# Gated linear attention, top-1 experts and a gated MLP: steps around the last head pair in another order, and widths by count for the first expert

## The chip, the cores and the metric

The kernel runs on one NeuronCore of a Trainium2 chip. The metric is the device time of one execution in microseconds (us), a median of three runs. The core has TensorE (PE, with its weight loads shown apart as PEld), VectorE (DVE), ScalarE (ACT), GpSimd (POOL) and the sync engine (SP), which only issues DMAs.

## The reference

```python
# 4 batches x 8 heads, 768 steps, head dim 48
for t in range(S):
    state = alpha[:, :, t, :, None] * state + np.einsum('bhd,bhe->bhde', k[:, :, t], v[:, :, t])
    y[:, :, t] = np.einsum('bhd,bhde->bhe', q[:, :, t], state)
x = y as (3072 tokens, 384)
# 8 experts, each token to one of them
logits = x @ w_gate
expert_idx = np.argmax(logits, axis=1); gate_w = softmax(logits)[expert_idx]
h = np.maximum(xe @ w1[e], 0.0); out[mask] = gate_w[mask, None] * (h @ w2[e])   # D=384, F=1024
# a second MLP over all tokens
h = x @ w_in; g = h * (1.0 / (1.0 + np.exp(-h))); result = g @ w_out            # 384 -> 2048 -> 384
```

All inputs and outputs are float32. With the reference's inputs, experts 0 to 7 get 420, 387, 356, 354, 404, 409, 352 and 390 tokens.

## The kernel before, in words

The program order on each engine is written out by hand; nothing is rescheduled. Eight PSUM banks (0 to 7) are given out by number.

**Attention.** The 32 heads are 16 pairs `p` (four to a batch), and the 768 steps are six chunks of 128. The loop over `p` runs to 16; each pass begins pair `p` and ends pair `p - 1`. For a pair, `scores` (tile `Ap`) and a mask give the part within a chunk; `ks_transpose` and `updates` give each chunk's update of the state; `states(p)` scans these on VectorE (tile `So`) and ScalarE copies the result to `Sb`; `from_states` and `within` add both parts up in PSUM (tile `Yp`, two halves of three chunks), and `y_copy(p, 0)` and `y_copy(p, 1)`, the "sums", copy the halves to `xb`. Named places in the pass (`"F1"`, `"F2"`, `"F3"`, `"U"`, `"C1"`, `"C2"`) take further steps from a table, through `aside(p, place)`. After the last pair of a batch, `logits(b)` multiplies the batch's `xb` with the gate's weights (tile `Lp`): eight fp32 matmuls, recorded as 16 passes, in four groups of 32 columns of the array. The sixth and the eighth of the matmuls read the last pair's halves. `route(b)` then finds each token's expert.

**Experts.** Tokens of an expert are gathered from DRAM (`xg`), transposed (`x_tile`, `x_rows`) and split into a high part `xh` (ScalarE) and a low part `xl` (VectorE). Weights come as tiles of 128x768, t = 0 to 7 for expert 0, and so on; `w_split(t)` casts one on ScalarE to `wh` and subtracts on VectorE or GpSimd to `wl`. A slice's first product `F1` is nine matmuls (hi·hi, lo·hi, hi·lo for three parts of the rows) into a bank `hp`; ScalarE makes `hh`, VectorE `hl` from it, and nine matmuls of `S1` add to three banks `yb` (two of them are also called `both`). Expert 0 goes in two passes: slices 0 to 5 on its first 192 columns, whose tokens come from the first three batches, while the last batch is being routed; then

```python
seq = [(t, CA, CAPS[0]) for t in range(part)] + [(t, 0, CAPS[t // NF]) for t in range(part, E * NF)]
```

that is, columns 192 to 448 of slices 0 to 5, slices 6 and 7 on all 448, and then the other experts, larger ones first. Slices of `seq` go in pairs; the first products run one slice ahead.

For experts 1 to 7, `sized(e, body)` loads the expert's count into a register of TensorE and chooses by comparisons, one after the other, among four widths (`ARMS[e]`); each width has its own copy of the matmuls. Expert 0 has no such choice: it runs at 448. Columns of `hp` that a narrower arm doesn't write have to be zero, so `hold()` takes three banks for good and clears them, after the sixth slice of `seq`:

```python
HB[0] = -1
for i in HBS:
    t = bank(i, [128, CAP], "hp")
    nc.vector.memset(t, 0.0)
    held.append(t)
```

At the end of the attention loop (`p` = 16), the steps stand in this order: `x_rows` of the first two gathered tiles, `within`, `y_copy(15, 0)` on ScalarE, `y_copy(15, 1)` on VectorE, `w_split(2)`, `w_split(3)`, `logits(3)`.

Of the kernel before, what the change touches and what calls it, by code (L numbers as in the profile page):

```python
# [9 lines left out]
F32 = mybir.dt.float32  # L10
# [12 lines left out]
NP = B * H // 2  # L23
# [15 lines left out]
ARMS = [  # L39
    [448],  # L40
    [420, 432, 444, 464],
# [198 lines left out]
def gla_moe_kernel(  # L240
# [87 lines left out]
    def w_load(t):  # L328
# [9 lines left out]
        nc.sync.dma_start(raw[t], wt[ds(wbase[r] + f, 1)].rearrange("o p f -> (o p) f"))  # L338

    def w_split(t, eng=nc.vector):  # L340
        hi, lo = wslot[slot1(t)]
        nc.scalar.copy(hi, raw[t])  # L342
        eng.tensor_tensor(lo, raw.pop(t), hi.bitcast(F32), op=ALU.subtract)  # L343

# [40 lines left out]
    turn = const.tile([128, E, E], F32, name="turn")  # L385
    regs = const.tile([128, 24], I32, name="regs")

# [11 lines left out]
    with actx:  # L399
# [252 lines left out]
        def states(p):  # L652
# [9 lines left out]
            if 0 < p < NP - 1:  # L662
                y_copy(p - 1, 0)
            for h in range(2):
                r = slice(64 * h, 64 * h + D)
                dst = Sb[p % 2][r, 1:NC, 64 * h : 64 * h + D]
                src = so[r].rearrange("p e c -> p c e")[:, 1:NC, :]
                if p == NP - 1 and h:
                    nc.vector.tensor_copy(dst, src)
                else:  # L670
                    nc.scalar.copy(dst, src)
# [33 lines left out]
        def y_copy(p, g):  # L705
            b, i = p // 4, p % 4
            if g == 0 and i == 0:
                xb[b] = xp.tile([PA, 4, S], F32, tag="xb", name="xb")
            c0 = 3 * g * CH
            dst, src = xb[b][:, i, c0 : c0 + 3 * CH], st[p]["y", g].rearrange("p c t -> p (c t)")  # L710
            if p == NP - 1 and g:
                nc.vector.tensor_copy(dst, src)
            else:
                nc.scalar.copy(dst, src)

# [250 lines left out]
        def beside_pairs(b):  # L966
# [23 lines left out]
            else:  # L990
# [7 lines left out]
                    (p + 2, "F2"): [invert, add, gather_a],  # L998
                    (p + 2, "C2"): [lambda: w_split(0, nc.gpsimd), lambda: w_split(1), lambda: w_load(4)],
                }  # L1000
# [28 lines left out]
        for p in range(NP + 1):  # L1029
# [49 lines left out]
            if not on:  # L1079
                x_rows(XG[0], XS[0], 0, 0, 128, bank(2, [128, KD, 128], "xt"))  # L1080
                x_rows(XG[1], XS[0], 1, 0, CA - 128, bank(0, [128, KD, 128], "xt"))
            if oy:
                within(p - 1, 0)
                within(p - 1, 1)
            if p < NP - 1:
                states(p)
            if p >= NP - 1:
                y_copy(p - 1, 0)
            if oy:
                y_copy(p - 1, 1)  # L1090
# [9 lines left out]
            if not on:  # L1100
                w_split(2)
                w_split(3)
                logits(B - 1)
# [20 lines left out]
    with mctx:  # L1124
# [126 lines left out]
        def hold():  # L1251

            HB[0] = -1
            for i in HBS:
                t = bank(i, [128, CAP], "hp")
                nc.vector.memset(t, 0.0)  # L1256
                held.append(t)

# [7 lines left out]
        def F1_inner(t, c0, c1):  # L1266
# [7 lines left out]
            )  # L1274
            hq[t, c0] = (hh, hl)

        yb = {}
# [51 lines left out]
        for t in range(part):  # L1329
            if t == 2:  # L1330
                add()
                w_split(4)
                gather(0, (1, 2, 3))
                for t_ in yb.values():
                    nc.vector.memset(t_[:, CAPS[0] :], 0.0)  # L1335
            if t == 3:
# [10 lines left out]
            if t == 0:  # L1347
                row[5]()
                for step in placed:
                    step()  # L1350
        x_tile(0, 3, bk=3)
        for t in range(4, 6):
            next_load()
        soon = [6, 7]
        HB[0], HBS[:] = -1, [5, 6, 3]
        F1(*seq[0])
        lctx.close()
# [9 lines left out]
        def offsets():  # L1367
# [7 lines left out]
            nc.vector.tensor_copy(regs[:, 9:16], cnt[:, 1:E])  # L1375

        count = {}

        def sized(e, body):

            if e not in count:
                c = 8 + e if e else 8
                count[e] = nc.values_load(regs[0:1, c : c + 1], engines=(ET.PE,), min_val=0, max_val=NT)

            def arm(i):
                if i == len(ARMS[e]) - 1:
                    body(ARMS[e][i])
                    return
                with tc.If(count[e] <= ARMS[e][i]) as cmp:
                    body(ARMS[e][i])  # L1390
                with cmp.Else():
                    arm(i + 1)

            arm(0)

# [154 lines left out]
        for i in range(0, len(seq), 2):  # L1550
# [4 lines left out]
            for e in sorted({t // NF for t, _, _ in todo}):  # L1555
                mine = [x for x in todo if x[0] // NF == e]
                if e == 0:
                    for x in mine:
                        F1_products(*x)
                else:  # L1560

                    def firsts(w):
                        for t, c0, c1 in mine:
                            F1_products(t, c0, w)

                    sized(e, firsts)
            F1_inner(*seq[i + 1])
# [30 lines left out]

            if e == 0:
                for g, c0, c1 in pair:  # L1600
                    S1_products(g, c0, c1, inner[g])
            else:
                sized(e, seconds)
            if i + 2 < len(seq):
                F1_inner(*seq[i + 2])
            else:
                F2_inner(0)
            if i == NF - 4:
                hold()
            if g1 % NF == NF - 1:  # L1610
# [105 lines left out]
```

## Time and profile before

| | |
|---|---|
| median of 3 runs | 762.66 us (762.14 to 763.0) |
| the profiled execution | 761.62 us, its span 759.6 us |
| granted TensorE clock | 1.00 of full speed in the stretches shown |
| PE busy | 745.3 us, 98% of the span |
| DVE busy | 466.8 us, 61% |
| ACT busy | 367.3 us, 48% |
| POOL busy | 167.0 us, 22% |

The span is the time from the first to the last recorded instruction; the profiled execution's own time is 2.0 us longer. Busy shares are means over stages with different limits: attention takes about the first 128 us, the experts up to about 360 us, and the second MLP the rest.

### The profile page before, as it was taken

Reading aid. Unit: us, or ns where it says so; the run is one execution under the profiler, and the core shown is the slowest. Engines: PE = TensorE matmul, PEld = TensorE weight load, DVE = VectorE, ACT = ScalarE, POOL = GpSimd, SP = SyncE. Lnnn points to the kernel's source line nnn. Section 1 sums busy time; section 2 is a strip of 40 time slices with the busy share of each in tenths; the row PEclk is TensorE's granted clock in tenths of the full one; section 3 lists DMA queues with packets and bytes.
Section 4 is the critical chain, followed back from the end, with each engine's and each line's share of the span. In section 5 each row is a group of like instructions: output and inputs, shape, how many; then the busy total and the mean of one; then the engine's idle time right before and its main releaser. Section 6 shows DMA issues by size and latency. Waiting matters only on the chain. (4 is left out here: it accounts for less than half of the span.)

```text
span 759.6 us, 13436 instructions
## 1 busy us (share of the span) xinstructions
PE 745.3 (98%) x5018; PEld 682.3 (90%) x5018; DVE 466.8 (61%) x778; ACT 367.3 (48%) x684; POOL 167.0 (22%) x207
## 2 busy tenths in 40 slices
PE   8999999999999999999999999999999999999997
PEld 6887878899999999999999899899999989899996
DVE  8989986667877887888787423333342333334222
ACT  2656566445655555566444434444564545334222
POOL 6764322321333224112111200110020010002002
PEclk9999999999999999999999999999999999999999
DMA  9887883535566565654111200030031000001001
GB/s 242 214 223 209 233 271 105 183 111 155 176 202 198 167 205 175 193 189 148 63 42 37 79 13 6 11 104 19 1 96 37 19 19 24 2 1 42 0 1 46
DMA packets 41802, 80.98 MB, mean 107 GB/s; under 512 B 5696, under 2 KB 19999, under 8 KB 41704
## 3 DMA queue, kind: packets, MB, share of 16 engines
q1 hardware_dynamic: 37704, 67.60, 30.4%
q0 software_dynamic: 4000, 12.03, 4.9%
q8 instruction: 67, 1.10, 0.6%
q14 instruction: 31, 0.25, 0.1%
HBM read 68.04 MB, written 9.47 MB: 102 GB/s over the span
## 5 line engine op out<-in xcount | busy, mean ns | idle before, releaser
L1232 PE MATMUL hp<-xh,wh 128*128 128x512 f32 (+10 forms) x498 | 180.4, 365 | 1.1 <-DVE hp L1256 0.7
L1232 PE MATMUL hp<-xh,wl 128*128 128x512 f32 (+10 forms) x498 | 180.3, 364 | 0.4 <-DVE wl L343 0.4
L1495 DVE TENSOR_TENSOR sg<-hp,sg 128x512 f32<-128x512 f32 (+1 forms) x97 | 66.4, 685 | 128.5 <-ACT sg L1494 128.0
L1232 PE MATMUL hp<-xl,wh 128*128 128x512 f32 (+10 forms) x498 | 127.4, 364 | 0.0
L1494 ACT ACTIVATE sg<-hp 128x512 f32<-128x512 f32 (+1 forms) x97 | 57.5, 593 | 118.4 <-PE hp L1232 113.4
L1232 PEld LDWEIGHTS hp<-xh,wh 128*128 128x128 f32 x498 | 93.6, 188 | 12.8 <-DVE hp L1256 0.9
L1232 PEld LDWEIGHTS hp<-xh,wl 128*128 128x128 f32 x498 | 93.6, 188 | 11.6 <-DVE wl L343 1.0
L1232 PEld LDWEIGHTS hp<-xl,wh 128*128 128x128 f32 x498 | 90.2, 188 | 11.9
L1540 POOL DMA_INDIRECT out_dram<-o,sidx x24 | 23.3, 973 | 275.4 <-ACT o L1538 270.9
L1159 POOL TENSOR_TENSOR wl<-dx,wh 128x384 fp32r<-128x384 f32 x32 | 39.1, 1221 | 168.1 <-ACT wh L1156 168.1
L343 DVE TENSOR_TENSOR wl<-raw,wh 128x768 fp32r<-128x768 f32 x63 | 65.1, 1037 | 10.9 <-ACT wh L342 10.6
L1270 ACT ACTIVATE hh<-hp 128x464 fp32r<-128x464 f32 (+9 forms) x70 | 34.0, 487 | 73.3 <-PE hp L1232 65.2
L1272 DVE SCALAR_TENSOR_TENSOR hl<-hp,hh 128x464 fp32r<-128x464 f32 (+9 forms) x70 | 37.8, 548 | 29.4 <-ACT hh L1270 29.2
L1506 DVE TENSOR_TENSOR hl<-sg,hh 128x512 fp32r<-128x512 f32 x49 | 33.9, 692 | 35.6 <-ACT hh L1505 34.2
L342 ACT CAST wh<-raw 128x768 fp32r<-128x768 f32 x64 | 52.0, 831 | 7.5 <-DMA raw<-in_wt_dram 7.3
L1505 ACT CAST hh<-sg 128x512 fp32r<-128x512 f32 x49 | 30.4, 621 | 49.9 <-DVE sg L1495 38.2
L1506 DVE TENSOR_TENSOR xl<-sg,xh 128x512 fp32r<-128x512 f32 (+1 forms) x48 | 32.7, 681 | 31.7 <-ACT xh L1505 23.3
L1296 PE MATMUL both<-hh,wh 128*128 128x396 f32 (+9 forms) x140 | 47.7, 341 | 0.3 <-DVE yb L1335 0.3
L1296 PE MATMUL both<-hl,wh 128*128 128x396 f32 (+9 forms) x140 | 46.0, 329 | 0.3 <-DVE hl L1272 0.3
L1505 ACT CAST xh<-sg 128x512 fp32r<-128x512 f32 (+1 forms) x48 | 29.3, 611 | 35.0 <-DVE sg L1495 35.0
L1296 PE MATMUL both<-hh,wl 128*128 128x396 f32 (+9 forms) x140 | 45.8, 327 | 0.0
L357 POOL DMA_INDIRECT xg<-x_d,gidx x29 | 34.5, 1188 | 42.1 <-PE xt L367 19.5
(367 smaller groups left out, 1645.9 us busy)
## 6 DMA issues: line engine op xcount, KB each, us to landing
raw<-in_wt_dram SPq DMA_DIRECT2D x64, 384.0 KB, 3.6
raw<-in_w_dram SPq DMA_DIRECT2D x32, 384.0 KB, 3.9
raw<-in_alpha_dram SPq DMA_DIRECT2D x16, 336.0 KB, 3.3
x_d<-xr SPq DMA_DIRECT2D x24, 192.0 KB, 2.2
E<-in_q_dram SPq DMA_DIRECT2D x18, 144.0 KB, 4.7
E<-in_k_dram SPq DMA_DIRECT2D x18, 144.0 KB, 2.8
E<-E POOLq DMA_DIRECT2D x18, 114.0 KB, 6.0
E<-in_q_dram SPq DMA_DIRECT2D x4, 336.0 KB, 8.6
```

What stands on the lines that cost most here:

```text
L342: nc.scalar.copy(hi, raw[t])
L343: eng.tensor_tensor(lo, raw.pop(t), hi.bitcast(F32), op=ALU.subtract)
L357: nc.gpsimd.indirect_dma_start(out=x[:n], out_offset=None, in_=src, in_offset=bass.IndirectOffsetOnAxis(ap=idx[:n, i : i + 1], axis=0),)
L1159: nc.gpsimd.tensor_tensor(r["lo"], r["x"], r["hi"].bitcast(F32), op=ALU.subtract)
L1232: nc.tensor.matmul(hp, lhsT=a[:, kc * 128 : (kc + 1) * 128], rhs=x[:, kc, c0:c1], start=(i == 0), stop=(i == 8))
L1270: nc.scalar.activation(hh[:, :n], hp, AF.Relu)
L1272: nc.vector.scalar_tensor_tensor(hl[:, :n], in0=hp, scalar=0.0, in1=hh[:, :n].bitcast(F32), op0=ALU.max, op1=ALU.subtract)
L1296: nc.tensor.matmul(yb[dc][:, c0:c1], lhsT=a[:, c : c + 128], rhs=b_[:, : c1 - c0], start=(f == 0 and c0 == 0 and i == 0), stop=(f == NF - ...
L1494: nc.scalar.activation(sg[:, z], hp[:, z], AF.Sigmoid)
L1495: nc.vector.tensor_tensor(sg[:, z], hp[:, z], sg[:, z], op=ALU.mult)
L1505: nc.scalar.copy(hh[:, z], sg[:, z])
L1506: nc.vector.tensor_tensor(hl[:, z], sg[:, z], hh[:, z].bitcast(F32), op=ALU.subtract)
```

## The change

It has six parts. (1) `w_split` is cut into `w_cast` (ScalarE) and `w_rest` (the subtraction); casts 0 and 1 move from place C2 of `p` = 15 to F3, ahead of the Sb copy, casts 2 and 3 from `p` = 16 to C2 of `p` = 15. (2) The last sum, too, is copied by ScalarE. (3) For `p` = 4, 8 and 12 the second sum of the pair before is copied ahead of the copies of the states. (4) The three banks are taken and cleared before the first slice of `seq`, from column 176 on (they hold columns from 192 of expert 0 first); with that `x_tile(0, 3)` changes its bank. (5) Expert 0 gets six arms. Its count goes to column 24 of `regs`. (6) The memset of the `yb` banks is 96 columns wide and no longer 16, and comes after the first slice of `seq`.

```diff
-    [448],
+    [368, 384, 400, 416, 432, 448],
...
+    def w_cast(t):
+        nc.scalar.copy(wslot[slot1(t)][0], raw[t])
+
+    def w_rest(t, eng=nc.vector):
+        hi, lo = wslot[slot1(t)]
+        eng.tensor_tensor(lo, raw.pop(t), hi.bitcast(F32), op=ALU.subtract)
...
                 y_copy(p - 1, 0)
+                if p % 4 == 0:
+                    y_copy(p - 1, 1)
             for h in range(2):
...
-            if p == NP - 1 and g:
-                nc.vector.tensor_copy(dst, src)
-            else:
-                nc.scalar.copy(dst, src)
+            nc.scalar.copy(dst, src)
...
-                    (p + 2, "C2"): [lambda: w_split(0, nc.gpsimd), lambda: w_split(1), lambda: w_load(4)],
+                    (p + 2, "F3"): [lambda: w_cast(0), lambda: w_cast(1)],
+                    (p + 2, "C2"): [
+                        lambda: w_rest(0, nc.gpsimd),
+                        lambda: w_rest(1),
+                        lambda: w_load(4),
+                        lambda: w_split(2),
+                        lambda: w_cast(3),
+                    ],
...
                 x_rows(XG[1], XS[0], 1, 0, CA - 128, bank(0, [128, KD, 128], "xt"))
+                w_rest(3)
...
-            if oy:
+            if oy and (p % 4 or p == NP):
                 y_copy(p - 1, 1)
...
             if not on:
-                w_split(2)
-                w_split(3)
                 logits(B - 1)
...
             for i in HBS:
-                t = bank(i, [128, CAP], "hp")
-                nc.vector.memset(t, 0.0)
-                held.append(t)
+                held.append(bank(i, [128, CAP], "hp"))
+            for t in held:
+                nc.vector.memset(t[:, min(ARMS[0]) - CA :], 0.0)
...
+                nc.vector.tensor_copy(regs[:, 24:25], carry[:, 0:1])
                 w_split(4)
                 gather(0, (1, 2, 3))
-                for t_ in yb.values():
-                    nc.vector.memset(t_[:, CAPS[0] :], 0.0)
...
-        x_tile(0, 3, bk=3)
+        HBS.append(3)
+        hold()
+        x_tile(0, 3)
...
-        HB[0], HBS[:] = -1, [5, 6, 3]
-        F1(*seq[0])
+        F1_bank(*seq[0][0:2])
+        sized_firsts(0, seq[0:1])
+        F1_inner(*seq[0])
+        for t in yb.values():
+            nc.vector.memset(t[:, min(ARMS[0]) :], 0.0)
...
-            if e == 0:
-                for g, c0, c1 in pair:
-                    S1_products(g, c0, c1, inner[g])
-            else:
-                sized(e, seconds)
+            sized(e, seconds)
...
-            if i == NF - 4:
-                hold()
```

`sized` itself is unchanged but for the column of the count; `sized_firsts(e, mine)` runs the nine matmuls of `F1` for each slice in `mine` through it. The rows below show where instructions stand on an engine: the line, the operation, and the tiles it writes and reads.

On ScalarE, around the logits of the first batch (pair 4 has begun), before:

```order
L714 COPY xb_441<-Yp_664 112x384
L671 COPY Sb_0_171<-So_709 48x5x48 x2
L714 COPY xb_441<-Yp_671 112x384
L745 COPY l_751<-Lp_742 128x384
L592 COPY kst_757<-Tp_753 128x336
```

and now:

```order
L719 COPY xb_441<-Yp_664 112x384
L719 COPY xb_441<-Yp_671 112x384
L679 COPY Sb_0_171<-So_709 48x5x48 x2
L750 COPY l_751<-Lp_742 128x384
L598 COPY kst_757<-Tp_753 128x336
```

The copy of the second sum has moved past the two copies of the states.

On ScalarE, at the last pair and the end of the attention loop (`wh0` to `wh3` are the casts, `xh0` the first gathered tokens), before:

```order
L592 COPY kst_1893<-Tp_1910 128x224
L671 COPY Sb_1_172<-So_1928 48x5x48
L714 COPY xb_1716<-Yp_1895 112x384
L714 COPY xb_1716<-Yp_1914 112x384
L342 CAST wh0_98<-raw_1507 128x768
L342 CAST wh1_100<-raw_1509 128x768
L371 CAST xh0_107<-xt_1968 128x3x128
L371 CAST xh0_107<-both_1974 128x3x64
L714 COPY xb_1716<-Yp_1961 112x384
L342 CAST wh2_102<-raw_1608 128x768
L342 CAST wh3_104<-raw_1610 128x768
L745 COPY l_2007<-Lp_1998 128x384
```

and now:

```order
L598 COPY kst_1893<-Tp_1910 128x224
L341 CAST wh0_98<-raw_1507 128x768
L341 CAST wh1_100<-raw_1509 128x768
L679 COPY Sb_1_172<-So_1930 48x5x48
L719 COPY xb_1716<-Yp_1895 112x384
L719 COPY xb_1716<-Yp_1914 112x384
L341 CAST wh2_102<-raw_1608 128x768
L341 CAST wh3_104<-raw_1610 128x768
L377 CAST xh0_107<-xt_1971 128x3x128
L377 CAST xh0_107<-both_1977 128x3x64
L719 COPY xb_1716<-Yp_1964 112x384
L719 COPY xb_1716<-Yp_1967 112x384
```

Casts 0 and 1 stand ahead of the Sb copy, casts 2 and 3 where 0 and 1 stood, and the last sum's copy (the last row) is on this engine.

On VectorE, from the last tiles of expert 0's tokens (`xl0`) to the second slice of `seq`, now:

```order
L378 TENSOR_TENSOR xl0_108<-xt_2293,xh0_107 128x3x64
L378 TENSOR_TENSOR xl0_108<-xt_2308,xh0_107 128x3x128
L1268 MEMSET hp_2323 128x288
L1268 MEMSET hp_2324 128x288
L1268 MEMSET hp_2325 128x288
L378 TENSOR_TENSOR xl0_108<-xt_2329,xh0_107 128x3x64
L1300 UNCONDITIONAL_BRANCH x2
L1283 SCALAR_TENSOR_TENSOR hl_2420<-hp_2323,hh_2418 128x256
L1397 MEMSET both_1977 128x96 x2
L1397 MEMSET yb_2115 128x96
```

Before, the three rows of `xl0` stood together, and the memsets of `hp` (128x464) came after the `hl` of the seventh slice of `seq`; both groups of memsets are at new places.

On TensorE, at the first slice of `seq`, now:

```order
L1333 MATMUL yb<-hl,wh_2027 128x192
L373 MATMUL xt<-identr,xg_2042 128x64 [waits DMASW6_49,DVE_49]
L373 MATMUL xt<-identr,xg_2042 128x64 x2
L1294 TENSOR_LOAD regs [waits DVE_49]
L1294 ISA x2
L1300 COMPARE_AND_BRANCH
L1243 MATMUL hp<-xh_107,wh_98 128x176 [waits DVE_49,Activation_49]
L1243 MATMUL hp<-xh_107,wl_99 128x176
```

Before, the matmuls (`hp<-xh_107,wh_98 128x256`) followed the transposes (`xt`) directly; now a value load and a chain of comparisons stand between them, and the transposes wait for VectorE as well as for the gather.

## Rows read from the trace of the kernel before

**Rows 1.** Windows: stretch in us, busy us of each engine, clock, DMA share, GB/s.

```profile
20.00:105.00 85.00, 83.31 (x1144) 69.09 (x1143) 81.43 (x112) 53.16 (x109) 48.48 (x59) 1.00 0.84 229
```

**Rows 2.** Timeline of weight loads: start, us, engine, line, operation; logits of the first batch.

```profile
45.33 0.12 PEld L731 LDWEIGHTS Lp<-xb,wgs 112*32 112x32 f32 x3 [0.20 <-issue]
46.01 0.14 PEld L731 LDWEIGHTS Lp<-xb,wgs 112*32 112x32 f32 x2 [0.56 <-ACT xb L714]
46.77 0.29 PEld L589 LDWEIGHTS Tp<-ident,E 112*128 112x128 f32 x3 [0.62 <-issue]
```

**Rows 3.** Timeline of ScalarE ahead of these logits.

```profile
44.18 1.28 ACT L671 COPY Sb<-So 48x240 f32<-48x240 f32 x2 [0.45 <-DVE So L654]
45.48 0.48 ACT L714 COPY xb<-Yp 112x384 f32<-112x384 f32 x1
```

**Rows 4.** Timeline of VectorE, behind the logits of the first three batches.

```profile
48.79 0.20 DVE L756 TENSOR_TENSOR lg<-lg,Lt 128x48 f32<-128x48 f32 x1 [1.15 <-ACT lg L755]
...
77.87 0.96 DVE L607 TENSOR_TENSOR Am<-Ap,mask 128x768 f32<-128x768 f32 x1 [0.37 <-PE Ap L601]
...
84.31 0.96 DVE L607 TENSOR_TENSOR Am<-Ap,mask 128x768 f32<-128x768 f32 x1 [0.27 <-PE Ap L601]
...
106.25 0.96 DVE L607 TENSOR_TENSOR Am<-Ap,mask 128x768 f32<-128x768 f32 x1 [0.38 <-PE Ap L601]
```

**Rows 5.** Timeline of weight loads, logits of the last batch.

```profile
128.28 0.12 PEld L731 LDWEIGHTS Lp<-xb,wgs 112*32 112x32 f32 x3 [0.20 <-issue]
129.40 0.14 PEld L731 LDWEIGHTS Lp<-xb,wgs 112*32 112x32 f32 x2 [1.00 <-DVE xb L712]
130.16 0.19 PEld L1232 LDWEIGHTS hp<-xh,wh 128*128 128x128 f32 x1 [0.62 <-issue]
```

**Rows 6.** Timelines of ScalarE and VectorE ahead of them.

```profile
122.74 0.63 ACT L671 COPY Sb<-So 48x240 f32<-48x240 f32 x1 [1.75 <-DVE So L654]
...
127.45 1.57 ACT L342 CAST wh<-raw 128x768 fp32r<-128x768 f32 x2
...
128.81 0.54 DVE L712 COPY xb<-Yp 112x384 f32<-112x384 f32 x1
```

**Rows 7.** Timelines of TensorE and VectorE, first pass of expert 0.

```profile
140.84 0.33 PE L1296 MATMUL both<-hh,wh 128*128 128x192 f32 x1 [0.28 <-DVE yb L1335]
...
145.35 0.42 PE L367 MATMUL xt<-identr,xg 128*128 128x128 f32 x3 [0.28 <-DMA xg<-x_d,gidx]
...
148.87 0.39 PE L1232 MATMUL hp<-xh,wh 128*128 128x256 f32 x1 [0.41 <-ACT xh L371]
...
146.93 0.35 DVE L372 TENSOR_TENSOR xl<-xt,xh 128x192 fp32r<-128x192 f32 x1
147.60 0.56 DVE L372 TENSOR_TENSOR xl<-xt,xh 128x384 fp32r<-128x384 f32 x1 [0.32 <-ACT xh L371]
```

**Rows 8.** Timelines of TensorE and VectorE, end of expert 0's second pass.

```profile
164.61 0.28 PE L1296 MATMUL yb<-hh,wl 128*128 128x256 f32 x1
164.73 0.28 PE L1296 MATMUL yb<-hl,wh 128*128 128x256 f32 x1
165.73 0.47 PE L1232 MATMUL hp<-xh,wh 128*128 128x448 f32 x1 [0.71 <-DVE hp L1256]
166.03 0.36 PE L1232 MATMUL hp<-xh,wl 128*128 128x448 f32 x1
...
167.65 0.35 PE L1232 MATMUL hp<-xh,wh 128*128 128x420 f32 x1
...
165.23 1.43 DVE L1256 MEMSET hp<- 128x464 f32 x3 [0.17 <-DVE hl L1272]
```

**Rows 9.** Comparisons (all; one section's) and value loads: count, min/median/max ns, starts.

```profile
L1389 PEldq COMPARE_BRANCH  x171: 64/176/1434, 166.7 to 355.8; - x171
...
L1389 PEldq COMPARE_BRANCH  x4: 69/192/208, 333.9 to 334.6; - x4
...
L1383 PEldq TENSOR_LOAD <-regs x7: 302/308/485, 165.8 to 326.9; - x7
```

More of the change, by code (lines that the diff above doesn't have):

```diff
@@ L338, in w_load @@
         nc.sync.dma_start(raw[t], wt[ds(wbase[r] + f, 1)].rearrange("o p f -> (o p) f"))
+    def w_cast(t):
[3 more added lines that the diff above has]
+        eng.tensor_tensor(lo, raw.pop(t), hi.bitcast(F32), op=ALU.subtract)
     def w_split(t, eng=nc.vector):
-        hi, lo = wslot[slot1(t)]
-        nc.scalar.copy(hi, raw[t])
-        eng.tensor_tensor(lo, raw.pop(t), hi.bitcast(F32), op=ALU.subtract)
+        w_cast(t)
+        w_rest(t, eng)
     XS, XG = [], []
@@ L385, in gla_moe_kernel @@
     turn = const.tile([128, E, E], F32, name="turn")
-    regs = const.tile([128, 24], I32, name="regs")
+    regs = const.tile([128, 25], I32, name="regs")
     def by_turn(x, m, res):
@@ L1275, in F1_inner, with sized, arm, sized_firsts @@
             hq[t, c0] = (hh, hl)
+        count = {}
+        def sized(e, body):
+            if e not in count:
+                c = 8 + e if e else 24
+                count[e] = nc.values_load(regs[0:1, c : c + 1], engines=(ET.PE,), min_val=0, max_val=NT)
+            def arm(i):
+                if i == len(ARMS[e]) - 1:
+                    body(ARMS[e][i])
+                    return
+                with tc.If(count[e] <= ARMS[e][i]) as cmp:
+                    body(ARMS[e][i])
+                with cmp.Else():
+                    arm(i + 1)
+            arm(0)
+        def sized_firsts(e, mine):
+            def firsts(w):
+                for t, c0, c1 in mine:
+                    F1_products(t, c0, w)
+            sized(e, firsts)
         yb = {}
@@ L1375, in offsets @@
             nc.vector.tensor_copy(regs[:, 9:16], cnt[:, 1:E])
[L1377 to L1394, printed above, removed]
         def read_offset(e):
@@ L1555, in gla_moe_kernel @@
             for e in sorted({t // NF for t, _, _ in todo}):
-                mine = [x for x in todo if x[0] // NF == e]
-                if e == 0:
-                    for x in mine:
-                        F1_products(*x)
-                else:
[L1562 to L1566, printed above, removed]
+                sized_firsts(e, [x for x in todo if x[0] // NF == e])
             F1_inner(*seq[i + 1])
@@ L1597, in seconds @@
                     S1_products(g, c0, w, inner[g])
-            if e == 0:
-                for g, c0, c1 in pair:
-                    S1_products(g, c0, c1, inner[g])
-            else:
-                sized(e, seconds)
+            sized(e, seconds)
             if i + 2 < len(seq):
```

## The prediction

> **What bounds the kernel now.** I read the busy times of the engines first (they stand in the table above): TensorE is busy in all but a few us, so an edit pays only where TensorE itself stands still or has fewer columns to run. [...] Then I went to the places where the diff's instructions stand, with the timeline of each engine, and asked which wait ends last there. All times below are made against the profiled execution (761.62 us, of which 759.6 are span); the median of the three runs is 1.04 us above it, so I take the differences to the median, 762.66.
>
> **Sums in front of states (first three batches).** A batch's logits are 16 passes in four column groups that run side by side, so four rounds of four. The weight loads show 3 in the round at 45.33 and then 2 at 46.01, after 0.56 us of idle until ScalarE's copy of the second sum [rows 2]. That copy sits behind two Sb copies of 1.28 us together [rows 3]. With the sum first, the last two passes join the rounds that are already running: the last load is at 45.33 and no longer at 46.01, so everything behind is 0.68, say 0.70 us, earlier. The Sb copies lose nothing: they begin after 0.45 us of idle for So, and the sum's copy (0.48) fits in there [rows 3]. The pattern stands twice more, at 72.3 and 100.7.
>
> How much of this reaches the end is VectorE's affair. Behind the first logits it is idle for 1.15 us until they arrive, so it can follow by the whole 0.70. Behind the second ones its only idle until the next batch are 0.37 and 0.27 us, each ended by a matmul of TensorE, and behind the third ones 0.38 [rows 4]: 0.64 and 0.38. Sum −1.7; bounds 0 (VectorE's 96% swallows it) and −2.1 (three times 0.70).
>
> **ScalarE copies all sums; casts of the last pairs.** In the last batch the loss is larger: 3 loads in the round at 128.28, 2 at 129.40 after 1.00 us of idle, and the first expert weights at 130.16, in both batches 0.76 us behind the last load [rows 2, 5]. The second sum is copied on VectorE, at 128.81, behind wl and xl work, while ScalarE runs two casts of 1.57 us together from 127.45 [rows 6]. After the change these casts stand ahead, and ScalarE copies the sum as soon as its matmuls are done, about 127.7; with the 0.48 of such a copy [rows 3] that is 128.2, in time for the loads of 128.28. So the last load comes at 128.28 instead of 129.40: −1.1. Bounds: −0.4 (the wait goes, but the two passes still run alone) and −1.15. The two casts that move up to p = 15 cost 1.57 us of ScalarE; they go into its 1.75 us of idle ahead of the Sb copy at 122.74 [rows 6]. Without that cover the Sb copy, and the sums behind it, would be late by up to 1.57 us; I take nothing. Casts 2 and 3 take the place that 0 and 1 had, and the subtractions (w_rest) only change places on VectorE and GpSimd: nothing.
>
> **Memset of the yb banks.** S1(0) starts at 140.84 after 0.28 us of idle for this memset. Moving it frees these and a restart (at 165.73, below, an idle of 0.71 costs 0.98), some 0.55 us; but 4.5 us later TensorE waits for gathered rows (145.35, idle 0.28) [rows 7], and when these land doesn't hang on S1. I take 0; bounds −0.55 and 0.
>
> **Held banks sooner.** At 165.73 the first matmul of width 448 comes 1.00 us after its forerunner, where 0.12 is usual, and its successor 0.30 later, where 0.20 is usual: three memsets of 464 columns (1.43 us) start only at 165.23 [rows 8]. That is 0.98 us lost, and it goes: the new memsets follow the xl of 147.60 (0.56 us), so stand at about 148.2, 288 columns or 0.30 us each (1.43 / 3 × 288 / 464). The first is done at 148.5, before its reader, which today starts at 148.87 on ScalarE's xh [rows 7]. The low part xl(0,3) now queues behind all three, to about 149.4; its reader is the seventh matmul from 148.87 on, at 149.6. Term −1.0; bounds −0.7 and −1.0.
>
> **Six arms: the widths.** The reference's inputs send 420 tokens to expert 0, so the arm is 432: four comparisons fail, the fifth holds. Of 144 matmuls 108 go from 256 to 240 columns and 36 from 448 to 432. Starts are 0.120 us apart at 256 columns and 0.2025 at 448 (166.03 to 167.65 holds eight) [rows 8], so 0.43 ns a column and 6.9 ns for 16: 1.0 us in all. Bounds −0.25 (only the wide ones follow the slope) and −1.0; I take −0.85.
>
> **Six arms: the branches.** Nine sections now begin with comparisons. A value load starts at 165.8 and its first comparison at 166.7, 0.9 us. Four comparisons of one section (three fail) span 333.9 to 334.6, so 0.23 us each or a little more; four failures cost about 1.05 [rows 9]. [...]
>
> The first section can't run ahead: TensorE's sequencer stands before it at transposes that wait for xl(0,1) on VectorE, done at 147.28 [rows 7]. 147.28 + 0.9 + 1.05 = 149.2, against 148.87 today: +0.35. The second section follows only 9 matmuls (1.1 us), and its chain with entry and exit is about 1.4 to 1.5: +0.45 with the restart. Together +0.8; bounds 0 (the chain runs beside the wait for xh) and +1.8 (one such jump as long as the longest in the trace, 1.43 us, and the 0.35). The seven other sections stand behind 18 matmuls of 0.118 us, 2.1 us of work for a chain of 1.5: hidden, with 0.55 us to spare. The before has 171 such comparisons, median 176 ns, nearly all hidden behind wider matmuls; I allow +0.4 for what sticks out, bounds 0 and +4.
>
> **Sum.** −1.7 − 1.1 + 0 − 1.0 − 0.85 + 0.8 + 0.4 = −3.45, so 762.66 becomes 759.2 (the profiled one 758.2).
>
> **The rivals.** A change of under 0.2% (1.5 us, so 761.1 to 764.2) can't be told from none.
>
> A, *the attention part is hidden*: VectorE, 96% busy, takes back what TensorE gains there, and only the other terms are left: −3.45 + 1.7 = −1.75, 760.9. For it: [rows 1]. Against it: the 1.15 us of idle in [rows 4], which is VectorE waiting for just these logits.
>
> B, *the branches of expert 0 aren't hidden* (the other side). Its matmuls are the narrowest of all, so the sequencer has the least lead, and each section jumps over arms that aren't run. If every jump costs what the longest did (1.43 us on top of the chain), each of the seven later sections loses 1.43 − 0.55, rounded to 0.85, and the first two 1.4 each: +8.75 on −4.65, so 766.8. If only each second one does, 762.8. It decides from 4.65 us lost in nine sections. For it: one comparison of 1434 ns. Against it: the median of 176 ns in 171. [...]
>
> C, *no stall at all*: the chains run beside other waits, and the yb memset pays too: −3.45 − 0.8 − 0.4 − 0.55 = −5.2, 757.5.
>
> D, *the arms don't do what they say*: the count is above 432, the widths stay: −3.45 + 0.85, 760.1.
>
> **How the numbers follow.** My forecast .60; A .17 (half of it inside 0.2%); B .12 (from 762.8 up: a third inside, two thirds slower); C .08; D .03. The range of 8 in 10 leaves out most of B and the far end of C: 756.8 to 762.8; the forecast's own is 757.8 to 760.9. Faster .60 + .085 + .08 + .03 = .79; same .085 + .04, .13; slower .08.
>
> **What would show it.** The last two logits loads of each batch in the round before them; VectorE's 1.15 us of idle at 48.79 cut to under 0.5; the first expert matmul about 2.8 us earlier than 130.17; no idle for hp at the 448-wide matmul, which is 432 wide; idle of PE ahead of the first two sections under 1 us together. Wrong it would be if the first expert matmul is only 1 us earlier (A), or if idle stands ahead of later sections of expert 0 (B).

## The result, and the profile after

The changed kernel takes 768.0 us (median of five, 765.63 to 770.94) against 762.48 us: 1.0074 times the time before, interval 1.0048 to 1.0100. It is 5.5 us slower; forecast were 3.45 us less. Its profiled execution took 767.68 us, with a span of 765.9.

The parts of the change that were priced as gains are there in the profile, though not all at once. Weight loads of the first batch's logits, and those of the third:

```profile
45.95 0.13 PEld L736 LDWEIGHTS Lp<-xb,wgs 112*32 112x32 f32 x4 [0.19 <-issue]
46.70 0.29 PEld L595 LDWEIGHTS Tp<-ident,E 112*128 112x128 f32 x3 [0.62 <-DMA a__717<-in_alpha_dram]
...
101.54 0.14 PEld L736 LDWEIGHTS Lp<-xb,wgs 112*32 112x32 f32 x4 [0.34 <-ACT xb L719]
101.92 0.14 PEld L736 LDWEIGHTS Lp<-xb,wgs 112*32 112x32 f32 x2 [0.24 <-ACT xb L719]
```

In the first batch the last four passes are one round (in [rows 2] there were three, and two more 0.68 us later), and so it is in the second. In the third they wait for ScalarE again. The logits themselves begin at other times than before: in this execution the weight loads behind the first ones come at 46.70, only 0.07 us earlier than in [rows 2], and those behind the third at 102.68, where the kernel before had 102.82. One profile doesn't show what this part gains; the run f_sums below does. VectorE's idle ahead of the first routing is 0.46 us where [rows 4] had 1.15:

```profile
48.73 0.20 DVE L761 TENSOR_TENSOR lg<-lg,Lt 128x48 f32<-128x48 f32 x1 [0.46 <-ACT lg L760]
```

At the last pair, a wait is new. Timelines of VectorE, GpSimd, TensorE and the weight loads (`hp<-xh,wh` are the first expert matmul's):

```profile
123.12 2.23 DVE L677 COPY Sb<-So 48x240 f32<-48x240 f32 x1
...
123.27 1.83 POOL L345 TENSOR_TENSOR wl<-raw,wh 128x768 fp32r<-128x768 f32 x1
...
125.50 0.77 PE L690 MATMUL Yp<-E,Sb 112*112 112x128 f32 x5 [1.47 <-DVE Sb L677]
...
129.41 0.15 PEld L736 LDWEIGHTS Lp<-xb,wgs 112*32 112x32 f32 x5 [0.18 <-ACT xb L719]
130.18 0.19 PEld L1243 LDWEIGHTS hp<-xh,wh 128*128 128x128 f32 x1 [0.62 <-issue]
```

The last logits lose nothing any more (one round of five loads at 129.41; in [rows 5] 1.12 us lay between the last two). But VectorE's copy of the state takes 2.23 us and ends 0.25 us behind GpSimd's subtraction beside it, and TensorE waits 1.47 us for it. So the first expert weights come at 130.18, where [rows 5] had 130.16: of 2.8 us that were to be gained by then, none is left in this execution. This wait is a part of that; executions also differ by themselves, and the same attention code puts these weights at 130.16 in the profile of before and at 132.70 in that of h_held, a run below.

Behind that comes the first large loss. These are all rows of TensorE's timeline with idle ahead of them, from the first slice of the second pass on, then the first slices of width 432 and the first of expert 1:

```profile
149.11 0.35 PE L1243 MATMUL hp<-xh,wh 128*128 128x240 f32 x1 [1.26 <-DVE hp L1268]
150.90 0.35 PE L1243 MATMUL hp<-xh,wh 128*128 128x240 f32 x1 [0.55 <-issue]
154.11 0.35 PE L1333 MATMUL both<-hh,wh 128*128 128x240 f32 x1 [0.74 <-ACT xh L377]
157.03 0.37 PE L1243 MATMUL hp<-xh,wh 128*128 128x240 f32 x1 [0.66 <-issue]
160.25 0.37 PE L1333 MATMUL both<-hh,wh 128*128 128x240 f32 x1 [0.48 <-ACT xh L377]
163.48 0.37 PE L1243 MATMUL hp<-xh,wh 128*128 128x240 f32 x1 [0.95 <-issue]
...
168.72 0.45 PE L1243 MATMUL hp<-xh,wh 128*128 128x432 f32 x1
...
170.59 0.36 PE L1243 MATMUL hp<-xh,wh 128*128 128x420 f32 x1
```

The wait for the held banks of [rows 8] is gone, and the widths are 240 and 432. But nearly each section of expert 0 has idle ahead of it, and the pass takes 170.59 − 149.11 = 21.5 us, where it took 167.65 − 148.87 = 18.8 [rows 7, 8]. The memset named at 149.11 was done at 148.5; what ended last there were the comparisons (those of the first section: count, min/median/max ns, starts):

```profile
L1300 PEldq COMPARE_BRANCH  x5: 69/201/244, 147.8 to 148.9; - x5
```

So the first section came as forecast, at 149.1 for 149.2.

The second loss lies where nothing was changed. The same two matmuls of the second MLP, one of its third slice and its last, in TensorE's timeline before, after, and in the first experiment below (a_col8):

```profile
376.16 0.62 PE L1232 MATMUL hp<-xl,wh 128*128 128x512 f32 x2
...
753.93 0.34 PE L1518 MATMUL ob<-wh,xl 128*128 128x384 f32 x1
```

```profile
379.37 0.63 PE L1243 MATMUL hp<-xl,wh 128*128 128x512 f32 x2
...
760.22 0.34 PE L1540 MATMUL ob<-wh,xl 128*128 128x384 f32 x1
```

```profile
381.62 0.62 PE L1243 MATMUL hp<-xl,wh 128*128 128x512 f32 x2
...
759.39 0.34 PE L1540 MATMUL ob<-wh,xl 128*128 128x384 f32 x1
```

That is 377.77 us before, 380.85 after and 377.77 in the experiment. There is no wait in it and the granted clock is the same 1.00; the matmuls themselves follow each other more slowly, in stretches. Three rows of one stretch after:

```profile
571.11 0.33 PE L1540 MATMUL ob<-wh,hh 128*128 128x384 f32 x1
...
572.15 0.34 PE L1540 MATMUL both<-wh,xh 128*128 128x384 f32 x1
...
574.09 0.34 PE L1540 MATMUL ob<-wh,xl 128*128 128x384 f32 x1
```

From the first row to the second it is six matmuls, 173 ns each; from the second to the third eleven, 176 ns each. Before, the same eleven are 173 ns apart (567.43 to 569.33).

### The profile page after: what moved, and what is told of

The parts are those of the page before. It is cut to its first block, busy times and chain, and to the rows that moved or that the text cites. A ratio compares the mean times of both kernels' runs of the same rounds, so it can differ in the third digit from the quotient of the medians.

```text
span 765.9 us, 13499 instructions
## 1 busy us (share of the span) xinstructions
PE 746.8 (98%) x5018; PEld 683.6 (89%) x5018; DVE 467.4 (61%) x778; ACT 366.3 (48%) x685; POOL 163.6 (21%) x207
```

## The experiments

"Column 8", "one arm" and so on name versions built on the changed kernel. Times are medians; the ratio is to the kernel before, run on the same chip, whose median was between 760.9 and 762.8 us. An "arm" is one width of expert 0 with its copy of the code.

| run | what it is | us | before | ratio, 95% interval |
|---|---|---|---|---|
| a_col8 | changed, count in column 8 | 764.59 | 761.85 | 1.0025 (1.0010 to 1.0041) |
| b_wide | before, 25 columns | 766.37 | 761.85 | 1.0057 (1.0039 to 1.0074) |
| c_onearm | a_col8, one arm | 758.89 | 761.85 | 0.9968 (0.9952 to 0.9984) |
| d_norest | c_onearm, subtraction 0 on VectorE | 758.55 | 761.85 | 0.9959 (0.9945 to 0.9974) |
| e_twoarms | d_norest, two arms | 758.00 | 760.89 | 0.9962 (0.9949 to 0.9975) |
| f_sums | before, sums in front | 759.75 | 760.89 | 0.9986 (0.9973 to 1.0000) |
| g_last | before, parts at the last pair | 759.86 | 760.89 | 0.9986 (0.9977 to 0.9996) |
| h_held | before, banks held sooner | 759.88 | 760.89 | 0.9988 (0.9979 to 0.9996) |
| i_front | d_norest, six arms, first holds | 761.56 | 761.59 | 0.9993 (0.9972 to 1.0013) |
| j_back | d_norest, six arms, fifth holds | 764.25 | 761.59 | 1.0025 (1.0012 to 1.0038) |
| e2_twoarms | as e_twoarms | 758.14 | 761.59 | 0.9957 (0.9943 to 0.9971) |
| d2_onearm | as d_norest | 757.87 | 761.59 | 0.9953 (0.9937 to 0.9969) |
| k_pad64 | before, tiles moved by 64 bytes | 763.54 | 760.90 | 1.0033 (1.0019 to 1.0048) |
| l_x1 | before, second token tiles moved by 32 | 764.74 | 760.90 | 1.0049 (1.0030 to 1.0068) |
| m_w | before, seven weight tiles moved by 32 | 764.23 | 760.90 | 1.0038 (1.0020 to 1.0056) |
| n_late | e_twoarms, from the third section on | 756.84 | 760.90 | 0.9945 (0.9928 to 0.9963) |
| o_pad128 | before, tiles moved by 128 | 765.00 | 762.77 | 1.0039 (1.0022 to 1.0055) |
| p_x128 | before, second token tiles and those behind them moved by 128 | 764.86 | 762.77 | 1.0038 (1.0023 to 1.0052) |

**The 25th column.** The tile `regs` stands in front of nearly all others in a partition of SBUF; with 100 bytes instead of 96 everything behind it moves by 32 bytes. Theory: that slows the second MLP. Rival: something in the longer program does.

```diff
-    regs = const.tile([128, 25], I32, name="regs")
+    regs = const.tile([128, 24], I32, name="regs")
...
-                c = 8 + e if e else 24
+                c = 8 + e if e else 8
...
-                nc.vector.tensor_copy(regs[:, 24:25], carry[:, 0:1])
+                nc.vector.tensor_copy(regs[:, 8:9], carry[:, 0:1])
```

> The changed kernel with one difference: expert 0's count goes to column 8 of regs (free until the end) and no longer to a 25th column, so regs keeps its 96 bytes a partition and every tile that is allocated behind it keeps the address it had before the change (they had moved by 32 bytes). Theory (place of the tiles): the second MLP goes back to the pace of the kernel before, 196.8 ns from matmul to matmul where the changed kernel's profile has 198.3, so 2.9 us less over some 1,820 matmuls: 765.1 us. Rival (the longer instruction stream or a timing between engines slows the second MLP): nothing, 768.0.

764.59 us, and the stretch above is back at 377.77 us. (The expectations further down count it from one matmul later, 377.54.) The other way round, the kernel before with that one number changed:

```diff
-    regs = const.tile([128, 24], I32, name="regs")
+    regs = const.tile([128, 25], I32, name="regs")
```

> The kernel before with one difference: regs has 25 columns and no longer 24; the 25th is never used. Theory (place of the tiles): the second MLP alone gets slower by the 2.9 us of the changed kernel, 765.4 us, and its matmuls show stretches of 31 to 36 in which the spacing is some 4 ns longer. Rival (instruction stream or timing): nothing, 762.5.

766.37 us, 4.5 more. Windows from 400 to 740 us of the kernel before, of a_col8, of the changed kernel and of b_wide (the second column has TensorE's matmuls in brackets):

```profile
400.00:740.00 340.00, 340.00 (x1726) 309.83 (x1725) 133.23 (x203) 145.16 (x256) 24.96 (x45) 1.00 0.10 29
```

```profile
400.00:740.00 340.00, 340.00 (x1724) 309.60 (x1724) 137.26 (x212) 147.50 (x260) 24.98 (x44) 1.00 0.10 29
```

```profile
400.00:740.00 340.00, 340.00 (x1711) 308.24 (x1711) 136.07 (x210) 146.31 (x258) 24.96 (x44) 1.00 0.10 29
```

```profile
400.00:740.00 340.00, 340.00 (x1711) 308.24 (x1710) 135.22 (x206) 145.88 (x257) 24.89 (x44) 1.00 0.10 29
```

1726 and 1724 matmuls at the old place, 1711 and 1711 at the new one: it goes with the 25th column, not with the program. The rival is out. The other profiles say the same: from its first matmul of 512 columns to its last matmul the second MLP takes 400.7 us in all 13 that have the old place, whatever else differs in the program, and 402.7 to 404.3 us in the seven that have another. Of b_wide's 4.5 us, 3.1 are these; the rest is not located (its attention took longer in the profile, but attention that is the same code ends 2.5 us apart in the profiles of before and h_held, as said above).

**What about the place?** Five further runs of the kernel before with tiles moved, and nothing else.

```diff
# k_pad64: 40 columns; o_pad128: 56 columns
-    regs = const.tile([128, 24], I32, name="regs")
+    regs = const.tile([128, 40], I32, name="regs")
# l_x1; m_w has the same two pads around mk_slots(wB, 4, 11); p_x128 a pad of 32 columns ahead of mk_x
+        wB.tile([128, 8], F32, name="pad0")
         mk_x(wB, 1)
+        wB.tile([128, 24], F32, name="pad1")
```

> The kernel before with regs 40 columns wide, so that all tiles behind it move by 64 bytes a partition instead of 32. Theory (a tile that TensorE reads must begin at a multiple of 64 bytes): nothing, the time of before, 761.6 us, and a second MLP at 196.8 ns from matmul to matmul. Rival (any move of the tiles, or of one against the others, costs the same): 3 us and more slower, as with 32 bytes.

> The kernel before with only the second set of token tiles (xh1, xl1 and its gather buffers) moved by 32 bytes; all tiles else stay at their place, or at one 128 bytes on. Theory (moving data that doesn't begin at a multiple of 64 bytes is read more slowly): the second MLP has the slow stretches of the changed kernel, 31 to 36 matmuls long, and is 2.75 us slower: 764.3 us. Rival (the weights are what matters): 761.6.

> The kernel before with only the seven weight tiles 4 to 10 (high and low parts) moved by 32 bytes. Theory (moving data): nothing, 761.6 us. Rival (weights): slower, 1 us or more, in the stretches that read these seven of sixteen tiles.

> The kernel before with regs 56 columns wide, so that all tiles behind it move by 128 bytes a partition. Theory (what TensorE reads has to begin at a multiple of 128 bytes): the second MLP takes the 377.54 us between its first and last matmul of all versions at the old place, and the time is that of before, 760.9 us. Rival (it is the place itself, or the distance to the first token tiles, which stay, that was good): 1.8 to 3 us slower, as with 64 and 32 bytes.

> The kernel before with the second set of token tiles, and the last five weight tiles behind them, moved by 128 bytes, all others at their old place. Theory (a multiple of 128 bytes is enough, whatever the distance from one tile to another): 377.54 us for the second MLP, 760.9 us in all. Rival (the distance between tiles read together matters): slower by 1.8 to 3.5 us, and then the two runs that moved only some tiles by 32 bytes say nothing on which tiles matter.

All five are slower, by 2.1 to 3.8 us in the medians. The same windows of k_pad64 and o_pad128:

```profile
400.00:740.00 340.00, 340.00 (x1718) 308.43 (x1717) 134.96 (x205) 145.85 (x257) 24.89 (x44) 1.00 0.10 29
```

```profile
400.00:740.00 340.00, 340.00 (x1712) 308.11 (x1712) 133.87 (x203) 145.27 (x256) 24.86 (x44) 1.00 0.10 29
```

(l_x1 1710, m_w 1712, p_x128 1711.) So a beginning at a multiple of 64, or of 128 bytes can't be what makes the old place good: a move by that much keeps it. The theories of a multiple fell, both, and since moves by 128 bytes cost as much, l_x1 and m_w say nothing on which tiles matter. What is shown: every one of six other placements is slower; why the old one is good stays open. The kernel before holds a hint that the diff passes over: two tiles that nothing reads, `gap0` of 24 columns ahead of the first token tiles and `gap1` of 32 ahead of the first weight tiles. They do nothing but set places.

**The comparisons of expert 0.**

```diff
-    [368, 384, 400, 416, 432, 448],
+    [448],
```

> The changed kernel with the count in column 8 and one arm of 448 for expert 0: no comparison is run in its nine sections (one load of the count stays), the widths are those of before. Theory (the comparisons and jumps are what the sections lose): between the first slice of the second pass and the first slices of expert 1 the changed kernel falls behind by 3.35 us although it gains 1.0 there from the banks that are cleared sooner, so 4.35 less than the version with column 8: 765.1 - 4.35 = 760.8 us; no idle of TensorE for 'issue' before matmuls of expert 0. Rival (late casts of weights and tokens on ScalarE, 0.7 and 1.2 us of waits there, have a cause of their own): the waits for xh and wh stay, 763 or more.

758.89 us, 5.7 less than a_col8: the comparisons and their jumps are the largest loss. No idle with releaser "issue" is left in the second pass, and the waits for late casts go as well, so these were its consequence. In a_col8's profile, of its slowest execution (767.26 us), a lower clock adds to the loss: behind 1.45 and 0.47 us of idle at the first two sections the granted clock is 0.59 and 0.56 in the windows from 150 to 154 us, and once more 0.57 from 314 to 318, behind 0.9 and 0.6 us of idle. In the changed kernel's profile and in j_back's it stays at 1.00 through the second pass.

> As the version with the subtraction of slice 0 on VectorE, with the changed kernel's six arms (368, 384, 400, 416, 432, 448), of which the fifth holds after four failing comparisons. Theory (length of the chain): about 5.7 us slower than one arm in the median, with idle of TensorE ahead of most of the nine sections, and a spread of some us between runs, from stretches of half clock behind that idle. Rival (the sections lost their time to what GpSimd's subtraction brought): under 2 us slower than one arm.

764.25 us, against 757.87 of d2_onearm on the same chip: 6.4 us, where some 5.7 were expected; the rival is out. The spread came too (761.0 to 765.6 us), but not from a lower clock as far as is shown: the profile is of the slowest execution, at a granted clock of 1.00. Then the same six copies of the code with the arm that holds in front:

```diff
-    [448],
+    [432, 436, 440, 442, 444, 448],
```

> As the version with the subtraction of slice 0 on VectorE, with six arms for expert 0 that begin with the one that holds: 432, 436, 440, 442, 444, 448. One comparison is run in each section, as with two arms; the code of a section is as long as the changed kernel's, and the jump behind the first arm goes over five others. Theory (the length of the chain of failing comparisons): like two arms, 0.3 to 0.9 us faster than one arm. Rival (length of the code and the jump over it): like the six arms of the changed kernel, 5 us and more slower than two arms.

761.56 us: 3.7 us slower than one arm, though no comparison fails in a section, and 2.7 faster than with four failing ones ahead (of j_back and i_front the intervals just touch, at 1.0012 and 1.0013). Its idle rows and its first matmul of expert 1, and the comparisons from 146 to 168 us:

```profile
148.47 0.38 PE L1243 MATMUL hp<-xh,wh 128*128 128x240 f32 x1 [0.41 <-DVE hp L1268]
157.25 0.70 PE L373 MATMUL xt<-identr,xg 128*128 128x128 f32 x6 [0.79 <-issue]
160.68 0.37 PE L1243 MATMUL hp<-xh,wh 128*128 128x240 f32 x1 [0.64 <-issue]
164.38 0.41 PE L373 MATMUL xt<-identr,xg 80*128 80x80 f32 x3 [0.65 <-DVE wl L345]
167.83 0.46 PE L1243 MATMUL hp<-xh,wh 128*128 128x432 f32 x1 [0.91 <-issue]
169.69 0.35 PE L1243 MATMUL hp<-xh,wh 128*128 128x420 f32 x1
...
L1300 PEldq COMPARE_BRANCH  x16: 64/140/3447, 147.7 to 167.9; - x16
```

The pass takes 21.2 us, nearly the 21.5 of the changed kernel, with 16 comparisons recorded where that one has 44 (two to a section, the one that holds and the one with the jump behind its arm, against six). With one arm it takes 17.8 us, in d2_onearm's timeline:

```profile
145.79 0.39 PE L1243 MATMUL hp<-xh,wh 128*128 128x256 f32 x1 [0.41 <-ACT xh L377]
...
163.59 0.35 PE L1243 MATMUL hp<-xh,wh 128*128 128x420 f32 x1
```

One comparison took 3447 ns. The DMA queue that brings instructions moved five pieces in 148 to 168 us here, and one with one arm:

```profile
q8 instruction: 5, 0.08, 1.7%
```

```profile
q8 instruction: 1, 0.02, 0.3%
```

Four of the 16 comparisons are long, 2.69 to 3.45 us, and in the time of each one piece of instructions is fetched. The first of them, from 154.2 to 157.2 us, and the queue in the same stretch:

```profile
L1300 PEldq COMPARE_BRANCH  x1: 2877/2877/2877, 154.3 to 154.3; - x1
```

```profile
q8 instruction: 1, 0.02, 2.4%
```

They end at 157.19, 160.50, 164.21 and 167.64 us, and the last four idle rows above start within 0.2 us behind them (the one at 164.38 names `wl`, which was done at 164.08). So TensorE stands still there until a long comparison is done; that its jump waits for the fetch of its target is the author's reading, and no run shows which piece holds the target. The changed kernel has four long ones as well in the pass, 1.40 to 1.93 us, among its failing comparisons; in its trace a piece of 16,384 bytes starts 0.76 to 0.95 us ahead of each and is done 1.26 to 1.43 us before the comparison ends. With two arms (e2_twoarms, below) none in that stretch is over 304 ns.

So neither theory holds alone. By the medians more than half of the loss, 3.7 of 6.4 us, comes with the long code and the jump over it, the rest with the failing comparisons; in the profiled passes nearly all does (17.8 us with one arm, 21.2 here, 21.6 in j_back).

**Two arms.**

```diff
-    [448],
+    [432, 448],
```

> As the version with the count in column 8, one arm and the subtraction of slice 0 on VectorE, but with two arms, 432 and 448, so that one comparison stands ahead of each of the nine sections of expert 0 and holds for the count of 420. Theory (it is the length of the chain, four failing comparisons of some 0.25 us, that uses up the lead of TensorE's sequencer): one comparison is hidden nearly everywhere and the narrower widths gain their 0.85 us, so 757.7 us against 758.55 with one arm. Rival (the jump itself, over code that isn't run, costs at each section whatever the number of comparisons): some 0.65 us for each of nine sections, as with six arms (764.59 - 758.89 = 5.7 us in nine), so 763 to 764.

> The version with two arms (432, 448) again, now on one chip with one arm. Theory: 0.85 us less than with one arm, from 16 columns less in 144 matmuls. Rival (each section's one comparison and jump cost what the width gains): equal within 0.3.

> The version with one arm and the subtraction on VectorE again, the base of the three others on their chip: 3.3 us less than the kernel before, as on the other chip (0.9959 of it).

758.14 against 757.87 us on one chip: equal. The code of a section is short, and what its jumps cost and what 16 columns gain can't be told apart. Without comparisons in the first two sections:

```diff
+        early = [0, 0]
...
+            if e == 0 and early:
+                early.pop()
+                body(ARMS[0][-1])
+                return
```

> The version with two arms (432, 448) and the subtraction on VectorE, but the first two sections of expert 0, ahead of which TensorE's sequencer has no or little lead, run at 448 without a comparison; the load of the count stands ahead of the third. Theory (the two arms lost their width's gain there, about 0.5 us): 0.5 us under two arms and one arm, 757.4 us where before is 761.6. Rival (the other sections cost as much as their width gains): equal to one arm, 757.9.

756.84 us, 4.1 less than before on its chip (0.9945, 0.9928 to 0.9963). It beats both kernels, as one arm does; that it beats one arm (0.9953, 0.9937 to 0.9969, on another chip) is not shown.

**GpSimd beside VectorE.**

```diff
-                        lambda: w_rest(0, nc.gpsimd),
+                        lambda: w_rest(0),
```

> As the version with column 8 and one arm, and the subtraction of weight slice 0 at the last pair is run on VectorE instead of GpSimd. Theory (GpSimd's subtraction holds up VectorE's copy of the state beside it, 2.23 us against 0.41): the copy takes about 0.4 us again, TensorE's wait of 1.47 us for it goes, 1.4 us less: 759.4 us. Rival (VectorE then has too much to do ahead of the first slice, about 1 us more of subtraction): the first expert matmul waits for wl, nothing is gained, 760.8.

758.55 against 758.89 us: the rival is out, since the first expert matmul doesn't wait for `wl` in the profile, but a gain is not shown in the medians. The reason is that the two meet in some executions only. In c_onearm's profile they meet; in a_col8's, with the same order, GpSimd begins after the copy (two timelines):

```profile
123.83 2.21 DVE L677 COPY Sb<-So 48x240 f32<-48x240 f32 x1
...
123.98 1.82 POOL L345 TENSOR_TENSOR wl<-raw,wh 128x768 fp32r<-128x768 f32 x1
```

```profile
122.80 0.41 DVE L677 COPY Sb<-So 48x240 f32<-48x240 f32 x1
...
123.66 1.83 POOL L345 TENSOR_TENSOR wl<-raw,wh 128x768 fp32r<-128x768 f32 x1
```

2.21 us with, 0.41 without. A lower clock follows c_onearm's idle of 1.46 us for this copy. Windows of it (the third column from the end is the granted clock):

```profile
124.00:127.00 3.00, 1.54 (x21) 1.32 (x18) 2.97 (x3) 2.79 (x5) 1.80 (x1) 1.00 0.21 66
...
128.00:130.00 2.00, 2.00 (x21) 1.99 (x22) 2.00 (x4) 0.94 (x3) 0.00 (x0) 0.55 0.58 178
130.00:132.00 2.00, 2.00 (x20) 0.75 (x19) 0.37 (x1) 0.48 (x1) 0.00 (x0) 0.60 0.90 243
132.00:134.00 2.00, 2.00 (x21) 1.51 (x14) 0.00 (x0) 0.68 (x2) 0.00 (x0) 1.00 0.52 187
```

From 128 to 132 us the granted clock was 0.55 and 0.60, so TensorE lost some 1.7 us more (an estimate: two us at 0.55 and two at 0.60). c_onearm's eight times lie in two groups, 758.1 to 759.5 and 761.4 to 761.9; the profile is of the upper one (761.64).

**The parts that gain, alone.** Each on the kernel before; g_last also has the change's steps at the places F3 and C2.

```diff
# f_sums
+                if p % 4 == 0:
+                    y_copy(p - 1, 1)
...
-            if oy:
+            if oy and (p % 4 or p == NP):
# g_last
-            if p == NP - 1 and g:
-                nc.vector.tensor_copy(dst, src)
-            else:
-                nc.scalar.copy(dst, src)
+            nc.scalar.copy(dst, src)
...
-                w_split(2)
-                w_split(3)
# h_held
-                nc.vector.memset(t, 0.0)
+                nc.vector.memset(t[:, CAPS[0] - CA :], 0.0)
...
-        x_tile(0, 3, bk=3)
+        HBS.append(3)
+        hold()
+        x_tile(0, 3)
...
```

> The kernel before with one part of the change alone: for pairs 4, 8 and 12 the second sum of the pair before is copied ahead of the copies of the states. Theory (the last two passes of the logits run beside the others, and VectorE can follow): 0.7, 0.6 and 0.4 us less behind the three logits, 1.7 in all, 760.1 us against 761.85. Rival (attention is bound by VectorE, or ScalarE's copies of the states are late instead): 761.85 within 0.4.

> The kernel before with the parts of the change at the last pair alone: casts 0 to 3 moved up, the subtraction of slice 0 on GpSimd, ScalarE copies the last sum. Theory (GpSimd's subtraction now runs beside VectorE's copy of the last state and stretches it from 0.41 to some 2.2 us): TensorE waits about 1.5 us for that copy, the logits gain 1.1 us back, so 762.2 us against 761.85, and more where the clock falls behind the wait. Rival (VectorE's copy was late for another reason that these parts don't bring): the copy takes 0.4 us, and the 1.1 us are gained, 760.75.

> The kernel before with the three banks taken and cleared ahead of the first slice of the second pass, from the column on that expert 0 doesn't write, and nothing else. Theory: the idle of 0.71 us at the first 448-wide matmul and its restart go, 1.0 us less, 760.9 us against 761.85; the low part xl(0,3) behind the memsets isn't waited for. Rival (the wait only moves, to the first slice, since the transposes of the last gathered rows now need a bank that VectorE has to free): a new idle of 0.5 us or more at the first slice of the second pass and no gain, 761.85.

f_sums 1.1 us less (at its interval's edge), g_last 1.0, h_held 1.0; together 3.2 (added before rounding), and c_onearm, which has all three, 3.0. In g_last the rival came out: GpSimd's subtraction began at 124.74, after VectorE's copy (0.41 us), and it is VectorE's subtractions that are stretched beside it (two in 3.39 us; in d2_onearm, where none runs on GpSimd, three took 2.69):

```profile
123.55 0.41 DVE L675 COPY Sb<-So 48x240 f32<-48x240 f32 x1
...
124.87 3.39 DVE L345 TENSOR_TENSOR wl<-raw,wh 128x768 fp32r<-128x768 f32 x2
...
124.74 1.83 POOL L345 TENSOR_TENSOR wl<-raw,wh 128x768 fp32r<-128x768 f32 x1
```

## Why the prediction was wrong, by its steps

| step | forecast | measured |
|---|---|---|
| sums in front of states | −1.7 | −1.1 (f_sums) |
| last sum on ScalarE, casts moved | −1.1 | −1.0 (g_last) |
| held banks | −1.0 | −1.0 (h_held) |
| widths and branches of six arms | −0.85 + 0.8 + 0.4 | +6.4 (j_back less d2_onearm) |
| the 25th column | not named | +2.8 (changed 5.5 above its before, a_col8 2.7); b_wide +4.5 |

- **Six arms: the branches** failed. The step priced the seven later sections as "hidden, with 0.55 us to spare", since each stands behind 2.1 us of matmuls. The chain of comparisons was sized about right (the first section came at 149.1 for 149.2), but the jump wasn't in the sum: i_front has no failing comparison and still loses 3.7 us. The longest comparison was read as an outlier in a median of 176 ns. For expert 0, whose sections are the shortest and whose six copies make the code of each the longest, four of the nine sections have such a one (1.40 to 1.93 us in the changed kernel), and five instruction pieces come in 20 us instead of one. Rival B named this way, and its threshold of 4.65 us was passed. That its 766.8 us lies near the measured time is in part luck: by it every section has a long jump, four have one, and 2.8 us of the loss are the 25th column's.
- **The 25th column** was no step at all. "Its count goes to column 24" was told as a part of the change and priced at nothing without a word. It moved the address of nearly every tile and cost 3.1 us in a stage that the diff doesn't touch.
- **"The subtractions only change places: nothing"** was wrong in the executions in which GpSimd's subtraction meets VectorE's copy: 1.47 us of TensorE in the changed kernel's profile. The copy took 2.23 and 2.21 us (the changed kernel, c_onearm) beside GpSimd's 1.83 and 1.82, each recorded 0.15 us behind the copy's start, and 0.41 without one (a_col8, g_last); what holds it up isn't shown. The cover of the casts on ScalarE, 1.75 us of idle, held: 0.68 us of it are left ahead of the Sb copy in the changed kernel's profile.
- **Sums in front** was the right mechanism with a somewhat large size. The profile after shows the logits of the first two batches as forecast, and in the third ScalarE late with both sums. Whether VectorE took back the difference is not shown; the interval of f_sums (0 to −2.1 us) holds the forecast.
- **Last logits, held banks** were right within 0.1 us by the medians. **The widths** can't be told apart from their branches: with two arms the sum of both is 0.3 us against one arm, with six 6.4.

The terms give −1.1 − 1.0 − 1.0 + 6.4 + 2.8 = +6.1 us; measured were +5.5, within what the intervals leave.

## What to carry to other kernels

Price a branch by the code it jumps over, not only by the comparison: with short sections and six copies four of nine sections had a comparison of 1.40 to 1.93 us in the changed kernel's profile, and two arms cost nothing that shows where six cost 6.4 us. Look at every allocation that a diff touches, even a column of four bytes, and compare a stage that wasn't changed before and after: here 1711 matmuls instead of 1726 in 340 us, with no wait and the same clock of 1.00, went with the place of the tiles. When a step is moved, ask also which instruction of the other engine it will now run beside: here a copy of 0.41 us became one of 2.23.

## What the runs showed of the hardware

- The matmuls of the second MLP take 377.77 us at one placement of the tiles, whatever else the kernel has (before, a_col8), and 0.4% to 0.9% more (1710 to 1718 matmuls in 340 us instead of 1724 and 1726) at six others, moved by 32, 64 or 128 bytes. The property that makes the first one good isn't found.
- A comparison with its jump took up to 3447 ns with six copies of a section's code (i_front) and up to 304 ns with two (e2_twoarms, expert 0's pass); each of the four over 2.6 us in i_front's pass has the fetch of one instruction piece in its time.
- VectorE's copy of 48x240 took 0.41 us without a GpSimd subtraction beside it (a_col8, g_last), and 2.23 and 2.21 us where one of 1.83 and 1.82 us began 0.15 us behind it (the changed kernel, c_onearm).
- After 1.46 us of idle in c_onearm's profile the granted clock fell to means of 0.55 and 0.60 for two windows of two us and came back; after the 1.47 us of the changed kernel's profile it didn't (1.00 from 126 to 136 us).
